# Layer-norm roots of a linear-attention and MLP block: a power on GpSimd in place of logarithm, exponential and Newton step

## The chip, the core and the metric

The kernel runs on one core of a Trainium2 chip. A core has five engines with instruction queues of their own: TensorE (PE in the profile, with its weight loads shown apart as PEld), VectorE (DVE), ScalarE (ACT), GpSimd (POOL) and SyncE (SP, which issues most DMAs). Each engine works through its queue in order and waits on semaphores for the others. The metric is the device time of one launch in microseconds. The kernel before takes 401.57 us (median of 3 runs, 401.56 to 401.84).

## What is computed

The input x has 2048 tokens of 512 channels, in fp32. It is normalised once, and the result feeds a linear attention of 32 heads and an MLP with squared ReLU; both are added to x:

```python
def _layernorm(x, axis=-1, eps=1e-5):
    m = jnp.mean(x, axis=axis, keepdims=True)
    v = jnp.var(x, axis=axis, keepdims=True)
    return (x - m) / jnp.sqrt(v + eps)

phi = lambda t: jnp.where(t > 0, t + 1, jnp.exp(t)) + 1e-6     # on q and k
kv, z = einsum("bhsd,bhse->bhde", phi(k), v), einsum("bhsd->bhd", phi(k))
o = einsum("bhqd,bhde->bhqe", phi(q), kv) / (einsum("bhqd,bhd->bhq", phi(q), z)[..., None] + 1e-6)
attention = o.reshape(B, S, D) @ wo
mlp = square(relu(xn @ w1 + b1)) @ w2 + b2
out = x + attention + mlp                                       # xn = _layernorm(x)
```

## The kernel before, in words

The tokens are cut into 16 tiles of 128 tokens (numbers 0 to 15). Every fp32 product is made of three fp32r products of a high and a low part: ScalarE copies the value to the high part (names that end in h), and VectorE or GpSimd subtracts it from the value to make the low part (names that end in l).

The program has a first stage, up to about 100 us, that walks over the 16 tiles, and a second one that walks over pairs of blocks of columns, first for one half of the tokens and then for the other. In the first stage a tile i goes through these steps:

- `measure`: VectorE's bn_stats and bn_aggr (BATCH_NORM_STATS2 and BATCH_NORM_AGGREGATE in the profile, BN_STATS and BN_AGGR in the order) give mean and variance into `mv`.
- `roots`: the root of the variance is made into the small tile `y`. Tiles are grouped, so one call serves one, two or three tiles; there are 10 groups: (0), (1), (2), (3), (4,8,9), (5,10), (6,11), (7,12), (13,14), (15).
- `normalise`: VectorE finishes the root and writes the normalised tile `xp` with one TENSOR_SCALAR of 128x512 (subtract the mean, multiply by the root).
- TensorE transposes `xp` (tiles 0 to 7) through the identity matrix `ident`; ScalarE and VectorE split the result into `xs1h`/`xs1l` or `xs0h`/`xs0l`. Tiles 8 to 15 are transposed by small DMAs (`xg`) and VectorE.
- `project` multiplies by the keys' weights (`wkh`, `wkl`, made of the loaded `rk`) into a PSUM bank `ps`; `phi` and `parts` make the keys `pk`; `tokens` makes `tok`, whose low part is a GpSimd TENSOR_TENSOR of 128x512; `kx` multiplies `pk` by `tok` into four PSUM banks `acc`.

Before the first real product TensorE runs eleven warm-up products on a tile of zeros (`zb`).

Nothing of this is issued in the order in which the code stands. All calls are recorded (class `Program`), and `order()` then plans the queues: TensorE's row is kept as it was recorded, and so is everything up to the first `kx` (the program of tiles 0 and 1 and a part of 2 to 4). For the rest, a list scheduler (`play`) with costs written by hand gives each instruction of the other engines its place; it is repeated `ROUNDS` = 500 times from each random seed in `STARTS` with due times pressed towards TensorE's gaps, and the best plan is issued. In these costs a GpSimd `tensor_tensor` and a VectorE `tensor_tensor` of SBUF operands keep each other out, and a small GpSimd instruction counts about 0.2 to 0.3 us. All instructions are issued from line 349, so the profile is read by the names of the tiles.

ScalarE's function tables are loaded once at the start (line 393, `natural_log_exp_and_others`).

Of the kernel before, what the change touches and what calls it, by code (L numbers as in the profile page):

```python
# [11 lines left out]
AF = mybir.ActivationFunctionType  # L12
OP = mybir.AluOpType
AX = mybir.AxisListType

P = 128
# [63 lines left out]
class Program:  # L80
# [96 lines left out]

    ENGINES = ("tensor", "vector", "scalar", "gpsimd", "sync")
    DEEP, FAR = 4.0, 15.0
    STARTS = (6, 14)  # L180
    ROUNDS = 500

    def order(self):
# [36 lines left out]
        plain, best, found = [t.due for t in ts], None, []  # L220
        for start in self.STARTS:
            chance, back = random.Random(start), (8, 16, 4)[start % 3]
# [138 lines left out]
def kernel(  # L361
# [12 lines left out]
    nc = Program(tc.nc)  # L374
# [67 lines left out]
    def two(name):  # L442
        return work.tile([P, 2, 512], F32, name=name, tag=next_tag("x"))

    def four(name, tag, dt=F32, pool=None):
        return (pool or work).tile([P, TB, 512], dt, name=name, tag=tag)
# [7 lines left out]
    def gjc(ap):  # L454

        return ap.rearrange("p (j g c) -> p g j c", j=NJ, g=NJ)
# [48 lines left out]
    odds = keep.tile([P, P // 2], F32, name="odds")  # L505
    b1s, zc = odds[:, 16:16 + NF], odds[:, 32:32 + 2 * NJ].rearrange("p (u j) -> p u j", u=2)
    zb = keep.tile([P, P], F32, name="zb")
    eps = odds[:, :1]

    xr, xp, xg, tok, pk, kp = {}, {}, {}, {}, {}, {}  # L510

# [204 lines left out]
    def roots(tiles, st, mv, y):  # L716

        n = len(tiles)
        nc.scalar.activation(y[:, 1, :n], mv[:, :n, 1], AF.Ln, bias=eps)
        nc.scalar.activation(y[:, 0, :n], y[:, 1, :n], AF.Exp, scale=-0.5)  # L720

    def normalise(tiles, st, mv, y):

        n = len(tiles)
        var = mv[:, :n, 1]
        y0, u, r = (y[:, k, :n] for k in range(3))

        nc.vector.scalar_tensor_tensor(u, var, 1e-5, y0, op0=OP.add, op1=OP.mult)
        nc.vector.scalar_tensor_tensor(u, u, -0.5, y0, op0=OP.mult, op1=OP.mult)
        nc.vector.scalar_tensor_tensor(r, u, 1.5, y0, op0=OP.add, op1=OP.mult)  # L730
        for k, i in enumerate(tiles):
            o, src = xp[i], xr[i]
            if i >= NPE:

                o, src = o.rearrange("p g (j c) -> p g j c", j=NJ), gjc(src)
            nc.vector.tensor_scalar(o, src, mv[:, k, 0:1], r[:, k:k + 1], op0=OP.subtract, op1=OP.mult)
            if i in groups:
                regroup(*groups[i])

    def regroup(src, G):  # L740

        for r in range(NJ):
            for g in range(NJ):
                moves.append((G[32 * g:32 * (g + 1), r], src[32 * r:32 * (r + 1), g]))
        return G
# [311 lines left out]


    nc.vector.memset(zb, 0.0)
    nc.vector.memset(eps, 1e-5)  # L1060
    t, rk = two("x0"), four("rk", "r0")
    for i in range(2):
        load_x(i, t[:, i:i + 1])
# [48 lines left out]
    for t in two_tiles:  # L1112
        roots(*t)
    normalise(*two_tiles[0])
    heads_k(0)
    high, low, keep0 = transposed(0)
    high()
    heads_k(1)
    normalise(*two_tiles[1])

    nc.gpsimd.tensor_copy(x4[:, 0, :1], two_tiles[1][3][:, 2, :1])
# [8 lines left out]
    third = statistics(2)  # L1130
    keep0()
    roots(*third)
    keep1()
    rests_k("dve", 1)
    normalise(*third)
    rests_k("dve", 3)
    fourth = statistics(3)
# [35 lines left out]
    parts(0)  # L1173
    keep2()
    roots(*fourth)
    normalise(*fourth)
    phi_k(1, pks[1])
# [68 lines left out]
    for i in range(2, NT):  # L1246
# [9 lines left out]
        k = NPE if i + 1 == NPE else i + 2  # L1256
# [463 lines left out]
```

## Time and profile before

| | before |
|---|---|
| device time, median of 3 runs | 401.57 us (401.56 to 401.84) |
| device time of the profiled execution | 402.07 us |
| its span, first to last instruction | 400.4 us |
| PE busy | 392.6 us (98%), 1763 matmul records |
| PEld busy | 324.5 us (81%) |
| DVE busy | 353.5 us (88%), 577 instructions |
| ACT busy | 271.7 us (68%), 478 instructions |
| POOL busy | 49.5 us (12%), 68 instructions |
| DMA moved | 94.37 MB, mean 236 GB/s |
| granted TensorE clock, mean | 0.997 |

Of the 402.07 us, 400.4 lie in the span and 1.7 around it. Matmuls are pipelined: a record lasts some 0.39 us, but the next one starts 0.227 us after it, so the records overlap, and TensorE waits whenever two of them start further apart than that. A share of 98% alone doesn't tell how tight the row is; the starts do. Names in the views carry no numbers, so `ps` stands for any of four PSUM banks, `acc` for any of the other four, and `y` for the small tile of any group.

### The profile page before, as it was taken

How to read it: one execution, taken by the hardware profiler on the slowest of the kernel's cores; microseconds unless marked ns; L12 is line 12 of the kernel's file. 1: busy time of each engine (PE TensorE's matmuls, PEld its weight loads, DVE VectorE, ACT ScalarE, POOL GpSimd, SP SyncE). 2: the span in 40 equal slices, each digit the busy share in tenths (PEclk: the TensorE clock that was granted, in tenths of full speed). 3: DMA queues.
4: the chain of work that ended last, by engine and by line, in shares of the span. 5: the costliest groups of instructions: out<-in, count | busy, mean ns of one | idle time of the engine just before them, and what ended most of it. 6: DMA issues, size and time to landing. Idle time of an engine off the chain costs nothing.

```text
span 400.4 us, 5611 instructions
## 1 busy us (share of the span) xinstructions
PE 392.6 (98%) x1763; PEld 324.5 (81%) x1763; DVE 353.5 (88%) x577; ACT 271.7 (68%) x478; POOL 49.5 (12%) x68
## 2 busy tenths in 40 slices
PE   7999999999999999999999999999999999999994
PEld 6778888888888887888888888887888888888884
DVE  5899999999998998999999999879999679676884
ACT  5786777677778989999757553186867677455440
POOL 2232322320122444100000000000000000000000
PEclk9999999999999999999999999999999999999998
DMA  7872387979678997797545799999975589999434
GB/s 235 289 220 58 94 249 229 338 283 310 248 230 306 327 359 275 250 315 262 186 146 199 245 235 243 306 250 255 272 232 185 178 226 292 227 281 278 156 64 95
DMA packets 80770, 94.37 MB, mean 236 GB/s; under 512 B 39490, under 2 KB 50754, under 8 KB 80484
## 3 DMA queue, kind: packets, MB, share of 16 engines
q1 hardware_dynamic: 79556, 93.49, 76.2%
q10 hardware_dynamic: 1088, 0.26, 0.3%
q0 software_dynamic: 96, 0.26, 0.3%
q8 instruction: 14, 0.23, 0.2%
q14 instruction: 16, 0.13, 0.1%
HBM read 57.81 MB, written 34.08 MB: 230 GB/s over the span
## 4 chain that ended last, share of the span: by engine, by line
PE 59%; DVE 1%; issue 0%
PE ps L349 32%; PE acc L349 28%; DVE res L349 0%; DVE o L349 0%
## 5 line engine op out<-in xcount | busy, mean ns | idle before, releaser
L349 PE MATMUL ps<-s,ops 128*128 128x512 f32 x435 | 102.6, 390 | 0.0
L349 PEld LDWEIGHTS ps<-s,ops 128*128 128x128 f32 x435 | 81.6, 188 | 17.1 <-ACT s L349 0.3
L349 DVE TENSOR_TENSOR s<-rr,s 128x512 fp32r<-128x512 f32 x56 | 38.2, 690 | 13.5 <-ACT s L349 12.9
L349 ACT ACTIVATE s<-rr 128x512 fp32r<-128x512 f32 x56 | 34.9, 630 | 22.2 <-DVE s L349 10.2
L349 PE MATMUL acc<-s,ops 128*128 128x512 f32 (+1 forms) x210 | 47.9, 380 | 0.0
L349 PE MATMUL acc<-pk,tok 128*128 128x512 f32 x192 | 47.1, 394 | 0.0
L349 PEld LDWEIGHTS acc<-s,ops 128*128 128x128 f32 x210 | 38.3, 188 | 7.5
L349 PEld LDWEIGHTS acc<-pk,tok 128*128 128x128 f32 x192 | 35.5, 188 | 7.8 <-DVE pk L349 0.6
L349 PE MATMUL acc<-T,ops 128*128 128x512 f32 x168 | 41.3, 390 | 0.0
L349 PE MATMUL ps<-T,ops 128*128 128x512 f32 x168 | 40.9, 391 | 0.1
L349 PEld LDWEIGHTS acc<-T,ops 128*128 128x128 f32 x168 | 31.5, 188 | 6.9 <-ACT rr L349 0.4
L349 PEld LDWEIGHTS ps<-T,ops 128*128 128x128 f32 x168 | 31.4, 188 | 7.0 <-ACT rf L349 0.5
L349 POOL DMA_DIRECT2D out_dram<-res x2 | 1.5, 728 | 229.0 <-DVE res L349 226.4
L349 POOL TENSOR_TENSOR tok<-xp,tok 128x512 fp32r<-128x512 f32 x16 | 21.7, 1354 | 42.1 <-ACT tok L349 30.6
L349 PE MATMUL ps<-xs0h,ops 128*128 128x512 f32 x72 | 23.7, 390 | 0.0
L349 ACT ACTIVATE rr<-acc 128x512 f32<-128x512 f32 x23 | 13.4, 586 | 12.3 <-PE acc L349 12.3
L349 DVE STREAM_TRANSPOSE d<-d 128x1024 f32<-128x1024 f32 x16 | 19.8, 1240 | 1.7 <-ACT d L349 1.5
L349 POOL TENSOR_TENSOR ops<-s,ops 128x512 fp32r<-128x512 f32 x12 | 15.9, 1328 | 25.3 <-ACT ops L349 22.2
L349 PE MATMUL acc<-xs0h,ops 128*128 128x512 f32 x56 | 18.4, 390 | 0.0
L349 ACT ACTIVATE s<-rf 128x512 fp32r<-128x512 f32 x19 | 11.9, 629 | 8.4 <-DVE rf L349 4.9
L349 ACT ACTIVATE rr<-rr,odds 128x512 f32<-128x512 f32 x15 | 10.8, 721 | 9.7 <-DVE rr L349 9.5
L349 DVE TENSOR_TENSOR ops<-raw,ops 128x512 fp32r<-128x512 f32 (+1 forms) x22 | 15.0, 681 | 2.6 <-ACT ops L349 2.6
(169 smaller groups left out, 801.4 us busy)
## 6 DMA issues: line engine op xcount, KB each, us to landing
ops<-wd SPq DMA_DIRECT2D x84, 256.0 KB, 4.1
wd<-ops SPq DMA_DIRECT2D x35, 512.0 KB, 3.6
ops<-wd SPq DMA_DIRECT2D x21, 512.0 KB, 5.8
wd<-ops SPq DMA_DIRECT2D x28, 256.0 KB, 3.5
res<-in_A_x_dram SPq DMA_DIRECT2D x32, 128.0 KB, 6.5
out_dram<-res SPq DMA_DIRECT2D x26, 128.0 KB, 3.6
ops<-wdz SPq DMA_DIRECT2D x6, 512.0 KB, 6.2
x<-in_A_x_dram SPq DMA_DIRECT2D x5, 512.0 KB, 4.9
```

Source lines behind the costliest of these rows:

```text
L349: getattr(getattr(self.nc, t.engine), t.name)(*map(real, t.args), **{k: real(a) for k, a in t.kw.items()})
```

## The change

The roots are made by two GpSimd instructions for each group: the variance plus 1e-5 into plane 1 of `y`, and that to the power of -0.5, which stands in a column of constants (`root`), into plane 2. ScalarE's Ln and Exp, and the three small VectorE instructions of the Newton step at the head of `normalise`, are gone. The scheduler starts from one random seed instead of two, so each queue is planned anew; TensorE's row is the same one.

```diff
-    STARTS = (6, 14)
+    STARTS = (5,)
...
-    eps = odds[:, :1]
+    root = odds[:, :1]
...
     def roots(tiles, st, mv, y):
         n = len(tiles)
-        nc.scalar.activation(y[:, 1, :n], mv[:, :n, 1], AF.Ln, bias=eps)
-        nc.scalar.activation(y[:, 0, :n], y[:, 1, :n], AF.Exp, scale=-0.5)
+        nc.gpsimd.tensor_scalar(y[:, 1, :n], mv[:, :n, 1], 1e-5, None, op0=OP.add)
+        nc.gpsimd.tensor_tensor(out=y[:, 2, :n], in0=y[:, 1, :n], in1=root.to_broadcast([P, n]), op=OP.pow)
 
     def normalise(tiles, st, mv, y):
         n = len(tiles)
-        var = mv[:, :n, 1]
-        y0, u, r = (y[:, k, :n] for k in range(3))
-        nc.vector.scalar_tensor_tensor(u, var, 1e-5, y0, op0=OP.add, op1=OP.mult)
-        nc.vector.scalar_tensor_tensor(u, u, -0.5, y0, op0=OP.mult, op1=OP.mult)
-        nc.vector.scalar_tensor_tensor(r, u, 1.5, y0, op0=OP.add, op1=OP.mult)
+        r = y[:, 2, :n]
...
-    nc.vector.memset(eps, 1e-5)
+    nc.vector.memset(root, -0.5)
```

GpSimd's queue at the start of the program, before (`y_147` is the root's tile of token tile 1, `wkl` a low part of the keys' weights):

```order
L349 AFFINE_SELECT heads<-heads 128x128 x2
L349 MEMSET odds 128x1
L349 MEMSET odds 1x1
L349 MEMSET xp_154 128x1
L349 COPY x_167<-y_147 128x1
L349 MEMSET xp_154 128x1
L349 TENSOR_TENSOR wkl<-rk,wkh 128x512
L349 MEMSET xp_154 128x1
L349 TENSOR_TENSOR tok_253<-xp_154,tok_253 128x512
```

And now (`y_141`, `y_150` and `y_198` belong to token tiles 0, 1 and 2, `odds` holds the constant -0.5):

```order
L349 AFFINE_SELECT heads<-heads 128x128 x2
L349 MEMSET odds 128x1
L349 MEMSET odds 1x1
L349 TENSOR_SCALAR y_141<-mv_137 128x1
L349 TENSOR_TENSOR y_141<-y_141,odds 128x1
L349 TENSOR_SCALAR y_150<-mv_144 128x1
L349 TENSOR_TENSOR y_150<-y_150,odds 128x1
L349 MEMSET xp_146 128x1
L349 COPY x_162<-y_150 128x1
L349 MEMSET xp_146 128x1
L349 TENSOR_TENSOR wkl<-rk,wkh 128x512
L349 TENSOR_SCALAR y_198<-mv_194 128x1
```

The two groups of the first two tiles stand one behind the other at the head of the queue, and the third behind the split of a weight.

VectorE's queue around token tile 4, before (`xp_378` is written for tile 4 first, `mv_269`/`y_333` belong to the group (4,8,9), `k_310` and `pk_350` to the keys of tile 2):

```order
L349 TENSOR_TENSOR xs1l<-ps_67,xs1h 128x4x128
L349 SCALAR_TENSOR_TENSOR k_310<-ps_70,k_310 128x512
L349 BN_STATS st_347<-x_167 128x6
L349 BN_STATS st_347<-x_239 128x6
L349 BN_AGGR mv_360<-st_347 128x2 x2
L349 BN_STATS st_364<-x_167 128x6
L349 SCALAR_TENSOR_TENSOR y_333<-mv_269,y_333 128x3
L349 SCALAR_TENSOR_TENSOR y_333<-y_333 128x3 x2
L349 TENSOR_SCALAR xp_378<-x_167,mv_269,y_333 128x512
L349 SCALAR_TENSOR_TENSOR pk_350<-k_310,pk_350 128x512
```

And now (the same tiles are `xp_335`, `mv_260`/`y_321`, `k_296` and `pk_338`):

```order
L349 TENSOR_TENSOR xs1l<-ps_67,xs1h 128x4x128
L349 SCALAR_TENSOR_TENSOR k_296<-ps_70,k_296 128x512
L349 TENSOR_SCALAR xp_335<-x_162,mv_260,y_321 128x512
L349 BN_STATS st_341<-x_162 128x6
L349 BN_STATS st_341<-x_230 128x6
L349 BN_AGGR mv_352<-st_341 128x2 x2
L349 BN_STATS st_356<-x_162 128x6
L349 SCALAR_TENSOR_TENSOR pk_338<-k_296,pk_338 128x512
L349 TENSOR_SCALAR xp_335<-x_162,mv_352,y_360 128x512
```

Tile 4 is now normalised right behind the keys of tile 2, ahead of three bn_stats that stood in front of it before.

## The prediction

> **What bounds the kernel now.** I read the page first, then the chain that ended last, then TensorE's own waits, and last the timeline around each of these waits. The page:
>
> ```profile
> span 400.4 us, 5611 instructions
> PE 392.6 (98%) x1763; PEld 324.5 (81%) x1763; DVE 353.5 (88%) x577; ACT 271.7 (68%) x478; POOL 49.5 (12%) x68
> PE 59%; DVE 1%; issue 0%
> ```
>
> TensorE is busy for 98% of the span, and 59% of the span is one unbroken chain of its work. The chain in order of time shows how tight that row is:
>
> ```profile
> 156.13 22.09 PE ps L349 x96
> ...
> 219.01 9.52 PE ps L349 x42
> ...
> 392.94 0.02 issue
> ```
>
> From 156.1 to 392.9 us it is TensorE without a break: 42 matmuls in 9.52 us are 0.227 us each, the pace at which one starts after the other. The 7.5 us from 392.9 to the end (400.4) are the last blocks' additions and stores. TensorE's order is the same in both programs, and the queues' last part, from where they stand at 304 us now, is the same too, so this tail stays. What the change can win or lose is therefore TensorE's waiting ahead of its work and between its matmuls. Besides the start of the warm-up, the view of its waits names three (total us, times, longest):
>
> ```profile
> PE acc L349 <- DVE y L349: 0.7, 1, 0.7
> PE acc L349 <- DVE xp L349: 0.3, 1, 0.3
> PE ps L349 <- DVE xp L349: 0.2, 1, 0.2
> ```
>
> All three wait for normalised tiles or their roots, so they are the change's business: two stand in the head (6 to 8 us), one at 26 us. Here is the head, in order of time (start, duration):
>
> ```profile
> 4.44 0.18 DVE L349 BATCH_NORM_AGGREGATE mv<-st 128x2 f32<-128x6 f32 x1
> 5.24 0.18 DVE L349 BATCH_NORM_AGGREGATE mv<-st 128x2 f32<-128x6 f32 x1
> 5.50 0.35 DVE L349 SCALAR_TENSOR_TENSOR y<-y 128x1 f32<-128x1 f32 x2
> 5.89 0.55 DVE L349 TENSOR_SCALAR xp<-x,mv,y 128x512 f32<-128x512 f32 x1
> 6.58 0.63 PE L349 MATMUL acc<-ident,xp 128*128 128x128 f32 x4 [0.68 <-DVE y L349]
> 6.92 0.55 DVE L349 TENSOR_SCALAR xp<-x,mv,y 128x512 f32<-128x512 f32 x1
> 7.24 0.60 ACT L349 ACTIVATE xs1h<-acc 128x512 fp32r<-128x512 f32 x1 [0.74 <-PE acc L349]
> 7.53 0.66 PE L349 MATMUL acc<-ident,xp 128*128 128x128 f32 x4 [0.32 <-DVE xp L349]
> 7.94 0.97 PE L349 MATMUL ps<-wkh,xs1h 128*128 128x512 f32 x2
> ```
>
> The variance of tile 0 is there at 4.62 us (4.44 + 0.18). Logarithm, exponential and Newton step take until 5.85 (5.50 + 0.35); the tile is written from 5.89 on, transposed at 6.58, split by ScalarE at 7.24, and the first real product starts at 7.94. Tile 1 follows, written at 6.92 and transposed at 7.53. Everything from 4.62 on is one chain, in which each step waits for the one before.
>
> **The change part by part. The head.** It takes ScalarE's two and VectorE's three small instructions out of this chain and puts GpSimd's two in. No power on GpSimd is in this trace. The nearest rows are these (groups of POOL instructions, then two rows of its timeline):
>
> ```profile
> L349 POOL TENSOR_TENSOR tok<-xp,tok 128x512 fp32r<-128x512 f32 x16 | 21.7, 1354 | 42.1 <-ACT tok L349 30.6 <-DVE pk L349 4.9 <-DMA wd<-ops 3.4
> L349 POOL TENSOR_TENSOR ops<-raw,ops 128x256 fp32r<-128x256 f32 x6 | 5.6, 936 | 26.9 <-ACT ops L349 26.9
> L349 POOL COPY x<-y 128x1 f32<-128x1 f32 x1 | 0.2, 184 | 0.0
> L349 POOL TENSOR_SCALAR_AFFINE_SELECT heads<-heads 128x128 f32<-128x128 f32 x2 | 0.7, 341 | 0.1
> 1.60 0.75 POOL L349 TENSOR_SCALAR_AFFINE_SELECT heads<-heads 128x128 f32<-128x128 f32 x2
> 7.32 0.19 POOL L349 MEMSET xp<- 128x1 f32 x1 [4.78 <-PE acc L349]
> ```
>
> The add is priced as the one-column COPY, 0.18 us. For the power, the least is that COPY, 0.18, and the most the 512-column TENSOR_TENSOR, 1.35. A line through 936 ns at 256 columns and 1354 at 512 has 1.63 ns per column and 0.52 us at one column; I take 0.52, since the power is a two-input TENSOR_TENSOR of one column, and an arithmetic of its own on one column is likely to be small beside the fixed part. A GpSimd instruction that waits for the one before it loses 0.07 us (two dependent selects take 0.75, not 2 x 0.341). A start behind another engine costs 0.11 (the MEMSET at 7.32, behind transposes that end at 6.58 + 0.63 = 7.21); the way back to VectorE I put at 0.04, as between VectorE's own steps (5.50 + 0.35 to 5.89).
>
> Tile 0: 4.62 + 0.11 + 0.18 + 0.07 + 0.52 + 0.04 = 5.54, against 5.89 now: 0.35 us earlier. At the power's least (0.18) it would be 5.20, but VectorE is busy with tile 1's aggregate until 5.24 + 0.18 = 5.42, so the gain is at most 0.43. Tile 1 queues behind the first power: 5.50 + 0.18 + 0.07 + 0.52 + 0.04 = 6.31, against 6.92: 0.61 earlier. Since the first product waits for the split of tile 0, the head gives 0.35. Nothing else there holds it back: the four weight loads are issued between 1.7 and 3.2 us and take at most 5.3, so the last is in by 8.5, while the last copy starts at 9.3:
>
> ```profile
> L349 SPq DMA_DIRECT2D rk<-in_A_wqkv_dram x4: 432/432/432, 1.7 to 3.2; - x4
> DMA to landing us min/median/max: 3.4/4.4/5.3
> L349 ACT ACTIVATE wkh<-rk x4: 613/627/632, 5.9 to 9.3; 128x512 fp32r<-128x512 f32 x4
> ```
>
> Two small steps of VectorE take 0.35 us in the head's rows, 0.175 each. The Trainium skill, in GPSIMD Engine Reference, section Engine selection, speaks against the move: it leaves elementwise work to VectorE, since GpSimd is about twice as slow on two inputs. As an estimate from that rule, a power of 2 x 0.175 = 0.35 us would even let the head gain its cap, 0.43, instead of 0.35; no row here has a two-input GpSimd instruction of one column, so I stay with the line through the two that there are.
>
> **The wait at 26 us.**
>
> ```profile
> 21.98 0.18 DVE L349 BATCH_NORM_AGGREGATE mv<-st 128x2 f32<-128x6 f32 x1
> 22.66 0.68 DVE L349 SCALAR_TENSOR_TENSOR k<-ps,k 128x512 f32<-128x512 f32 x1
> 25.18 1.07 PE L349 MATMUL ps<-wkh,xs1l 128*128 128x512 f32 x4
> 25.88 0.55 DVE L349 TENSOR_SCALAR xp<-x,mv,y 128x512 f32<-128x512 f32 x1
> 26.49 0.66 PE L349 MATMUL ps<-ident,xp 128*128 128x128 f32 x4 [0.24 <-DVE xp L349]
> 26.90 3.00 PE L349 MATMUL acc<-pk,tok 128*128 128x512 f32 x12
> ```
>
> The four matmuls from 25.18 on start 0.227 apart, so the next could start at 26.09; tile 4's transposes start at 26.49, when its normalisation (25.88 + 0.55 = 26.43) is over: 0.40 us of TensorE's time. Its variance was there at 22.16. In the new order this normalisation follows the keys of tile 2 (now over at 23.34), and its root is made by GpSimd at about 22.16 + 0.11 + 0.18 + 0.07 + 0.52 = 23.04. So the tile is ready near 23.9, two microseconds ahead of the transposes, and the 0.40 goes. Late next is the low part of `pk` for tile 2, which now stands behind the normalisation and three bn_stats: 23.9, three times some 0.68 (the keys' row above stands for a VectorE pass over 512 columns) and two aggregates of 0.18 make 26.3, and with a pass of its own it ends at 27.0, while TensorE, 0.40 earlier, asks for it four matmuls after its start at 26.50, at 27.4. That holds.
>
> **The other eight groups** (the third and fourth, and the pairs) have their roots hidden: TensorE shows no wait for them, and what goes there is work beside TensorE's. Here are twenty of VectorE's thirty small steps, and the busy times from 30 to 60 us (PE, PEld, DVE, ACT, POOL):
>
> ```profile
> L349 DVE SCALAR_TENSOR_TENSOR y<-y x20: 151/160/164, 5.5 to 46.1; 128x1 f32<-128x1 f32 x10, 128x2 f32<-128x2 f32 x8, 128x3 f32<-128x3 f32 x2
> 30.00:60.00 30.00, 30.00 (x140) 24.82 (x139) 28.60 (x64) 20.88 (x45) 8.56 (x14) 1.00 0.48 134
> ```
>
> Those twenty cost 20 x 0.16 = 3.2 us in all. VectorE is nearly full there (28.60 of 30), so taking work off it loosens the plan, but TensorE is busy for all of the 30 us and gains nothing. GpSimd's new instructions stand in order between the low parts of `tok`, 1.35 us each, which wait for ScalarE; a root may wait for one or two of them, and VectorE then stands still in front of that tile. That is a new coupling. GpSimd is busy for 8.56 of 30 us there, so I cost it at nothing.
>
> **The re-planned stretch** from 60 to 300 us: the view of waits names none there, but the starts show a few short ones, such as the 0.26 us between these two rows (155.64 + 0.227 = 155.87, and the next starts at 156.13):
>
> ```profile
> 155.64 0.39 PE L349 MATMUL ps<-xs1h,ops 128*128 128x512 f32 x1
> 156.13 1.66 PE L349 MATMUL ps<-T,ops 128*128 128x512 f32 x6
> ```
>
> A new plan may lose these or have others; I take no difference, with estimated bounds of -0.8 (three waits of this size gone) and +1.5 (six new ones).
>
> Sum: -0.35 - 0.40 = -0.75 us; with the power's two ends it would be -0.43 - 0.40 = -0.83 and, as worked out with the first rival, 1.04 - 0.40 = +0.64. Against the profiled execution (402.07, of which 400.4 is its span) that is 401.3. The median of the runs lies 0.5 below that execution, so the forecast for the median is 401.57 - 0.75 = **400.8 us**. A measurement of this kernel can tell about 0.2%, 0.80 us, from no change, so the forecast lies almost on that bound.
>
> **The rivals.** *The power is slow, and tile 1 pays twice (slower).* Both roots of the head stand in series on GpSimd. With a power of p, tile 1 is written at 5.26 + 2p, against 6.92, and the first product stands behind tile 1's transposes in TensorE's row. From p = 0.83 on the head loses, 2p - 1.66 (1.04 at 1.35); with the 0.40 won back, the kernel is slower from p = 1.03 on, and by over 0.80 from p = 1.43. At p = 2 it is +1.9: 403.5. For it: a power has to be computed in steps, and no row shows its arithmetic. Against: 1.43 us for one column is more than 512 columns of a subtraction take. A load of code at first use would do the same once; the only load of this kind in the trace is ScalarE's table, 1.28 us:
>
> ```profile
> L393 ACT ACT_TABLE_LOAD x1 | 1.3, 1283 | 0.8 <-PEq L1706 0.8
> ```
>
> A load of that length would write tile 1 at 6.31 + 1.28 = 7.59, 0.67 later, and the kernel would be 0.27 slower. The same page of the Trainium skill (GPSIMD Engine Reference, section Instruction dispatch) gives about 6 us for the first call to freshly loaded code, unseen in the profile; with that figure it would be some 406. In this trace no first instruction of a kind on GpSimd shows such a gap (the first COPY and the selects above), and the changed program has no load instruction that the old one lacks.
>
> *Given back in the new plan.* The gain holds to 30 us, and new waits of TensorE between 60 and 300 us eat it: 401.2 to 402.2, or in a bad plan 402.5 to 403.2. For it: all queues are reshuffled, one seed instead of two. Against: the chain has no break in that stretch worth a line, and VectorE has less to do.
>
> *More goes.* The short waits go as well: 400.8 - 0.8 = 400.0. For it: most of them end with VectorE or ScalarE, both relieved. Against: the ones after 60 us have nothing to do with the roots.
>
> **How the numbers follow.** The forecast with its small spread (-0.45 to -1.1) has 0.42, half of it on each side of the bound of 0.80; more goes, 0.18; given back within the bound, 0.17; the slow power beyond it, 0.13; a bad plan, 0.10. Faster by over 0.2%: 0.21 + 0.18 = 0.39; within: 0.21 + 0.17 = 0.38; slower: 0.23. The range from 399.9 to 403.0 takes in the case in which more goes and the milder half of the slower cases, and leaves out about 2 in 10.
>
> **What would show it.** Right: the power at 0.4 to 0.6 us; the first real product near 7.6; no wait of PE for `xp` at 26 us; 42 matmuls in 9.5 us afterwards, and the same tail of 7.5. Wrong: a power over 0.8 us and a first product later than 7.94; a wait of PE for `pk` or `xs0h` between 26 and 60 us behind a root that stands behind `tok` on POOL; or waits of over 1 us in sum after 60 us.

## The result, and the profile after

The change makes the kernel slower: 403.21 us (median of 10 runs, 402.26 to 404.42) against 401.64 us for the kernel before (10 runs beside them, 401.44 to 403.31). The ratio is 1.0033, with a 95% interval from 1.0020 to 1.0047. The forecast was 400.8 us, with a range up to 403.0.

The profiled execution took 402.32 us (402.07 before), one of the fastest of its ten. Its page:

```profile
span 400.6 us, 5579 instructions
PE 393.1 (98%) x1763; PEld 324.4 (81%) x1763; DVE 352.2 (88%) x547; ACT 267.6 (67%) x458; POOL 60.9 (15%) x88
```

Work left VectorE and ScalarE as forecast, and the 88 GpSimd instructions are busy for 11 us more; TensorE is again busy for 98%. TensorE's waits (total us, times, longest):

```profile
PE ps L349 <- DVE odds L349: 1.1, 1, 1.1
PE ps L349 <- DVE rr L349: 0.7, 1, 0.7
PE acc L349 <- DVE xp L349: 0.4, 1, 0.4
```

The first row is the warm-up's start, as before, and the third is the head's second tile. The waits for `y` and for tile 4's `xp` are gone; one for `rr`, which the kernel before hasn't, is new. The head in order of time (start, duration):

```profile
4.22 0.18 DVE L349 BATCH_NORM_AGGREGATE mv<-st 128x2 f32<-128x6 f32 x1
4.59 0.23 POOL L349 TENSOR_SCALAR y<-mv 128x1 f32<-128x1 f32 x1 [2.02 <-DVE mv L349]
4.91 0.57 POOL L349 TENSOR_TENSOR y<-y,odds 128x1 f32<-128x1 f32 x1
5.47 0.21 POOL L349 TENSOR_SCALAR y<-mv 128x1 f32<-128x1 f32 x1
5.52 0.55 DVE L349 TENSOR_SCALAR xp<-x,mv,y 128x512 f32<-128x512 f32 x1 [0.32 <-POOL y L349]
5.76 0.73 POOL L349 TENSOR_TENSOR y<-y,odds 128x1 f32<-128x1 f32 x1
6.53 0.55 DVE L349 TENSOR_SCALAR xp<-x,mv,y 128x512 f32<-128x512 f32 x1 [0.46 <-POOL y L349]
7.54 0.94 PE L349 MATMUL ps<-wkh,xs1h 128*128 128x512 f32 x2
```

From the variance (4.40) to the first product (7.54) it is 3.14 us, against 3.32 before (4.62 to 7.94): 0.18 gained, and 0.22 more because x landed earlier in this execution. At 26 us (TensorE, in order of time):

```profile
24.79 1.07 PE L349 MATMUL ps<-wkh,xs1l 128*128 128x512 f32 x4
25.70 0.60 PE L349 MATMUL ps<-ident,xp 128*128 128x128 f32 x4
```

Four matmuls 0.227 apart from 24.79 end at 25.70, and tile 4's transposes start at 25.70: the 0.40 us are won as forecast. Not all of it stays: tile 4's normalisation took 1.52 us beside GpSimd's token addition (22.93 to 24.45, where the forecast had 23.9), and TensorE stands a moment for tile 2's `pk` (over at 27.03): 0.15 us goes again by 30 us.

The 1763 matmul records of the two kernels are the same products in the same order, so their starts can be compared one by one. TensorE is 0.85 us ahead of the kernel before behind 26 us, 0.70 at 30 us and 0.50 from 52 to 137 us. The rest is lost near 138 us. GpSimd, then VectorE, then TensorE there:

```profile
134.25 2.55 POOL L349 TENSOR_TENSOR ops<-s,ops 128x512 fp32r<-128x512 f32 x2 [2.39 <-ACT ops L349]
...
135.58 2.30 DVE L349 SCALAR_TENSOR_TENSOR rr<-rr,d 128x1024 f32<-128x1024 f32 x1
...
136.32 1.52 PE L349 MATMUL ps<-T,ops 128*128 128x512 f32 x6
...
137.80 0.68 DVE L349 SCALAR_TENSOR_TENSOR rr<-ps,rr 128x512 f32<-128x512 f32 x1
...
138.53 0.50 PE L349 MATMUL ps<-xs0h,ops 128*128 128x512 f32 x1 [0.69 <-DVE rr L349]
```

The step at 137.80 empties the PSUM bank that TensorE's next product writes. Before, it ran ahead of the wide steps:

```profile
135.97 0.69 DVE L349 SCALAR_TENSOR_TENSOR rr<-ps,rr 128x512 f32<-128x512 f32 x1 [0.21 <-ACT rr L349]
```

In the new queue the 1024 wide step stands in front of it, and takes 2.30 us beside GpSimd's additions. TensorE's six matmuls are over at 137.68 (136.32 + 6 x 0.227) and it stands until 138.53. From there it is 0.4 to 0.5 us behind the kernel before, so this place cost 0.98 us. Then two things nearly cancel: the kernel before loses 0.35 us at 268 to 275 us, to a wait that the experiments explain, and the changed kernel 0.26 at 330 us. At the end it is 0.2 behind.

### The profile page after: what moved, and what is told of

It is laid out like the page before. It is cut to its first block, busy times and chain, and to the rows that moved or that the text cites. A ratio compares the mean times of both kernels' runs of the same rounds, so it can differ in the third digit from the quotient of the medians.

```text
span 400.6 us, 5579 instructions
## 1 busy us (share of the span) xinstructions
PE 393.1 (98%) x1763; PEld 324.4 (81%) x1763; DVE 352.2 (88%) x547; ACT 267.6 (67%) x458; POOL 60.9 (15%) x88
## 4 chain that ended last, share of the span: by engine, by line
PE 91%; DVE 4%; ACT 1%; issue 1%; DMA 1%; POOL 0%; DVEq 0%; POOLq 0%
PE ps L349 52%; PE acc L349 40%; DVE rr L349 1%; DVE d L349 1%; DMA x<-in_A_x_dram 1%; DVE s L349 1%; ACT rr L349 0%; POOL y L349 0%; DVE res L349 0%; DVE o L349 0%; ACT ops L349 0%; ACT d L349 0%; DVE st L349 0%; DVE h L349 0%; ACT e L349 0%
## 5 line engine op out<-in xcount | busy, mean ns | idle before, releaser
L349 POOL TENSOR_TENSOR ops<-s,ops 128x512 fp32r<-128x512 f32 x12 | 16.9, 1414 | 26.0 <-ACT ops L349 23.2
L349 ACT ACTIVATE k<-ps 128x512 f32<-128x512 f32 x16 | 9.5, 596 | 11.2 <-PE ps L349 11.1
```

The source lines that it names most:

```text
L349: getattr(getattr(self.nc, t.engine), t.name)(*map(real, t.args), **{k: real(a) for k, a in t.kw.items()})
```

## The experiments

Times are medians, with the lowest and highest run. In each series the kernels ran on one chip, beside runs of the kernel before, whose median is given. The first and third series shared a chip, the fourth and fifth another, and the second had a third one, so a small difference between two series may be the chip's. Where TensorE is said to lose or gain in a stretch, the starts of the same products in two profiled executions are compared.

**First series (before: 401.84).** Is it the power or the new plan? One kernel has the power on the old plan, one the logarithm on the new:

```diff
 # old_plan_power: the order as planned before; at emission
-scalar.activation(y1, var, Ln, bias=eps);  scalar.activation(y0, y1, Exp, scale=-0.5)
+gpsimd.tensor_scalar(y1, var, 1e-5, None, op0=add);  gpsimd.tensor_tensor(out=y2, in0=y1, in1=root, op=pow)
-three vector.scalar_tensor_tensor of the Newton step
 # new_plan_log: the order as planned after; at emission the reverse
```

> The kernel before, every instruction where its plan puts it, but ScalarE's Ln gives way to GpSimd's add, its Exp to GpSimd's power, and VectorE's Newton steps are left out. Theory A (the new plan costs, the power itself pays): PE's first product 0.2 to 0.4 us earlier than in before, the wait at 26 us gone, no new wait of PE at 138 us; the time 0.3 to 0.7 us under before, near 401.1. Theory B (the power on GpSimd costs, in series or by delaying other work): slower than before by 1 to 1.6 us, near 403. Theory C (both by halves): within 0.3 us of before.

> The changed kernel's order of all other work, but with the roots as before: Ln and Exp on ScalarE in the places of the add and the power, and the three Newton steps on VectorE ahead of each group's first normalisation. Theory A: the wait of PE near 138 us (0.85 us in the changed kernel) is there again, and the time is slower than before by 1 to 2 us, 402.6 to 403.6. Theory B: within 0.4 us of before, since the power is gone.

The power on the old plan took 401.79 us (401.14 to 402.97), ratio 0.9998 (0.9987 to 1.0009): not slower, which tells against theory B, but without the 0.3 to 0.7 us of theory A either. Its trace has the first product 0.23 us earlier and no wait at 138 us; at 26 us half of the 0.40 is left (0.21), since tile 4's normalisation still stands behind the three bn_stats there. The logarithm on the new plan took 411.87 us (409.27 to 415.25). That is no clean test: ScalarE's two steps, put into GpSimd's places, lose 5.9 us by 52 us already. It does have the same wait for `rr` of 0.7 us at 138 us, with no power in it.

Two more kernels: the pair at 136 us exchanged, and the changed kernel again.

```diff
 # swap_138: VectorE's queue
-scalar_tensor_tensor rr<-rr,d    128x1024
 scalar_tensor_tensor rr<-ps,rr   128x512
+scalar_tensor_tensor rr<-rr,d    128x1024
```

> The changed kernel with two neighbours of VectorE's queue exchanged near 136 us: the 128x512 step that empties the PSUM bank goes ahead of the 1024 wide step. Theory A (that wait is a chief part of the loss): PE's wait of 0.85 us near 138 us falls under 0.2, and the time is 0.5 to 0.9 us under the changed kernel. Theory A2 (the loss has many places): the wait goes, and under 0.3 us of it arrives at the end, as later waits take it up.

> The changed kernel once more, beside the other three on one chip: 402.3 to 404.4 us, a median 1.2 to 1.8 us above before's. If its spread is of the plan, a slower execution's trace shows waits of PE that the first profile lacks; if it is of the chip, before spreads as much.

The exchange took 402.48 us (401.46 to 404.76), the changed kernel 404.37 (402.37 to 405.69), 2.5 over before, beyond its expectation. GpSimd and VectorE in the first of them:

```profile
134.46 2.54 POOL L355 TENSOR_TENSOR ops<-s,ops 128x512 fp32r<-128x512 f32 x2 [2.40 <-ACT ops L355]
...
136.53 0.69 DVE L355 SCALAR_TENSOR_TENSOR rr<-ps,rr 128x512 f32<-128x512 f32 x1 [0.78 <-ACT rr L355]
137.13 1.22 DVE L355 SCALAR_TENSOR_TENSOR rr<-rr,d 128x1024 f32<-128x1024 f32 x1
```

The wait at 138 us is gone, and the wide step, no longer beside GpSimd, takes 1.22 us. At 138 us TensorE has won 0.96 us on the changed kernel's first execution; a new wait of 0.6 us at 146 us takes part of it, of which half is made up by 160 us. The 1.9 us between the two medians are more than this and hold the spread told next. The second execution of the changed kernel (404.56 us) shows where its spread lies. It has the same loss at 138 us, and then VectorE's wait near 255 us and TensorE at 270 us:

```profile
DVE res L349 <- DMA res<-in_A_x_dram: 2.7, 1, 2.7
```

```profile
267.79 2.43 PE L349 MATMUL acc<-T,ops 128*128 128x512 f32 x10
270.59 1.65 PE L349 MATMUL acc<-T,ops 128*128 128x512 f32 x6 [0.37 <-ACT rr L349]
...
273.21 0.39 PE L349 MATMUL acc<-xs1h,ops 128*128 128x512 f32 x1
274.35 1.66 PE L349 MATMUL acc<-T,ops 128*128 128x512 f32 x6 [0.75 <-ACT rr L349]
```

VectorE stands for the last of eight residual loads (the x that is added to the output), the chain behind it is late, and TensorE loses 0.53 us (267.79 + 10 x 0.227 to 270.59) and 0.91 (273.21 + 0.227 to 274.35). The faster execution waited 0.4 us there, the kernel before 1.6:

```profile
DVE res L349 <- DMA res<-in_A_x_dram: 1.6, 1, 1.6
```

So this wait is in both plans, and differs from run to run.

**Second series (before: 401.88, 401.43 to 404.30).** It is meant to take that wait away. Three loads of the second residual tile stand ahead of the eight in SP's queue; they go behind them.

```diff
 # SP's queue near 236 us (the changed kernel's numbers; alike in the others)
-DMA res_2367<-in_A_x_dram x3
 DMA ops<-wd_0_79;  DMA res_2388<-in_A_x_dram x4;  DMA ops<-wd_0_79;  DMA res_2388<-in_A_x_dram
 DMA ops<-wdz;  DMA res_2388<-in_A_x_dram;  DMA ops<-wd_0_79;  DMA res_2388<-in_A_x_dram x2
+DMA res_2367<-in_A_x_dram x3
```

> The changed kernel with one exchange in SP's queue: the three loads of the second residual tile that stand ahead of the eight of the first (near 236 us) go behind the last of them. Theory R (what varies from run to run is the landing of the eighth, which VectorE waits for near 255 us and, through ScalarE's evictions, PE near 272 us): it lands 1 to 2 us earlier, PE's waits at 269 to 273 us go, the wait at 138 us (0.85) stays; 402.0 to 402.6 us with runs closer together, 0.6 to 1.2 under the changed kernel. Rival S (the spread is the DMA engines' rate as a whole): the delay shows in the next loads instead and the median stays near 403.5.

> The changed kernel with both exchanges: VectorE's pair at 136 us and SP's residual loads. Theory: with both waits gone the new plan is as good as the old, 401.2 to 401.8 us. Rival: the new plan has further losses, and it stays over 402.0.

> The kernel before with the same exchange in SP's queue. Theory R: its slower runs (402 to 403.2) come from the same landing and go; its median falls to 401.3 to 401.5, 0.2 to 0.5 under before. Rival S: no difference, spread as before.

> The old plan with the power in place, and the exchange in SP's queue. Theory R: the 0.5 us that the power gives at the head is kept to the end in every run: 400.7 to 401.2 us, 0.6 to 1.0 under before, and 0.4 to 0.6 under before with the exchange. Rival S: near 401.8, as without the exchange.

| with the residual exchange | us | lowest to highest |
|---|---|---|
| after_res: the changed kernel | 403.33 | 402.83 to 404.38 |
| swap_res: and VectorE's pair exchanged | 402.45 | 401.94 to 403.04 |
| before_res: the kernel before | 401.52 | 401.29 to 401.65 |
| old_plan_power_res: the power, old plan | 401.47 | 400.96 to 401.73 |

Before_res is as theory R has it: the spread falls from 2.9 to 0.4 us, the median by 0.36, and VectorE's wait at 255 us is not in its trace. The changed kernel keeps its loss, against theory R's 402.0 to 402.6: in its trace VectorE still waits 1.7 us for the last load and TensorE loses 0.6 at 271 to 275 us, so here the exchange did not do what it was made for. The power on the old plan lies only 0.05 under before_res, against theory R's 0.4 to 0.6.

The first two rows differ by the exchange at 136 us alone, 0.88 us by their medians; part of that may be the late load, for which swap_res waited only 0.3 us. Swap_res, in which theory said 401.2 to 401.8, is still 0.98 above the power on the old plan, as its rival had it. In the two traces TensorE loses 1.0 us at 49 to 52 us, 0.6 at 146 (0.4 of it made up by 158) and 0.2 at 330, against a lead of 0.4 in its execution at 48 us. The first of these places, VectorE and GpSimd in the changed kernel and then VectorE in the kernel before:

```profile
46.08 0.71 DVE L349 STREAM_TRANSPOSE xT<-xg 128x512 f32<-128x512 f32 x1 [0.49 <-DMA xg<-xp]
46.72 0.65 DVE L349 TENSOR_TENSOR xs0l<-ps,xs0h 128x512 fp32r<-128x512 f32 x1
47.30 0.67 DVE L349 SCALAR_TENSOR_TENSOR k<-ps,k 128x512 f32<-128x512 f32 x1
47.89 0.67 DVE L349 TENSOR_TENSOR xs1l<-xT,xs1h 128x512 fp32r<-128x512 f32 x1
48.48 0.70 DVE L349 STREAM_TRANSPOSE xT<-xg 128x512 f32<-128x512 f32 x1
49.11 1.35 DVE L349 SCALAR_TENSOR_TENSOR pk<-k,pk 128x512 fp32r<-128x512 f32 x1
48.60 1.31 POOL L349 TENSOR_TENSOR tok<-xp,tok 128x512 fp32r<-128x512 f32 x1 [1.29 <-ACT tok L349]
```

```profile
47.38 0.68 DVE L349 SCALAR_TENSOR_TENSOR k<-ps,k 128x512 f32<-128x512 f32 x1
...
48.88 0.68 DVE L349 SCALAR_TENSOR_TENSOR pk<-k,pk 128x512 fp32r<-128x512 f32 x1
...
50.42 0.71 DVE L349 STREAM_TRANSPOSE xT<-xg 128x512 f32<-128x512 f32 x1 [0.52 <-DMA xg<-xp]
```

The new plan puts the turn of gathered tokens (STREAM_TRANSPOSE), which waits for a DMA, ahead of the `pk` that TensorE waits for, and `pk` takes 1.35 us instead of 0.68 beside GpSimd's token addition. In the changed kernel and in swap_138 that cost 0.2 to 0.3 us; in after_res and swap_res the turn started 0.7 to 1.0 us later, and it cost 1.0 to 1.2. Why the gathered tokens came later there is not shown.

**Third series (before: 401.66).** The kernel after_three makes the third exchange as well (to the diffs above):

```diff
 # VectorE's queue near 46 us
-stream_transpose xT<-xg
 tensor_tensor xs0l<-ps,xs0h;  scalar_tensor_tensor k<-ps,k
-tensor_tensor xs1l<-xT,xs1h;  stream_transpose xT<-xg
 scalar_tensor_tensor pk<-k,pk
+stream_transpose xT<-xg;  tensor_tensor xs1l<-xT,xs1h;  stream_transpose xT<-xg
 # ScalarE's queue: xs1h<-xT goes behind pk<-k
```

> The changed kernel with three exchanges in queues and nothing else: SP's residual loads (236 us), VectorE's pair at 136 us, and at 46 to 50 us the first two turns of gathered tokens on VectorE and the split behind the first on ScalarE, which go behind the two steps (ScalarE's and VectorE's pk) that PE waits for at 51 us. Theory Q (the whole loss is instructions that stand in a queue ahead of a step for PE): the step of 0.3 to 1.2 us at 49 to 51 us goes as well, and the time is 0.3 to 1.0 us under the kernel with two exchanges (402.45), 401.4 to 402.0. Rival T (the exchange makes PE wait for the turned tokens a little later): within 0.3 of 402.45.

It took 402.62 us (402.24 to 403.03), no better than swap_res (402.45, on another chip). The loss at 51 us is gone (TensorE is 1.1 us earlier there than in swap_res), but 0.7 of it comes back at 56 us, as rival T had it. Swap_138, on the same chip, had lost only 0.3 at 51 us, and against it the third exchange costs 0.4 by 58 us. This part of the loss is found in the trace, not undone.

The next two change only the starting numbers of the plan's random search:

```diff
 # after_old_starts                # before_new_start
-STARTS = (5,)                    -STARTS = (6, 14)
+STARTS = (6, 14)                 +STARTS = (5,)
```

> The changed kernel's tasks, planned from the two starting numbers of the kernel before (6 and 14) instead of 5. Theory L (which waits a plan leaves is chance of its search; the power takes no part in them): other waits in other places, anywhere between 401.2 and 404. Rival M (the power's tasks make every plan worse): it too lies 1.3 us or more over before, with waits behind GpSimd's instructions.

> The kernel before, planned from the starting number 5. Theory L: a different plan with the logarithm is 0.3 to 2.5 us over before as well, though no power is in it. Rival M: within 0.4 us of before.

The changed kernel from the old numbers took 402.20 us (401.02 to 403.60), ratio 1.0006 (0.9994 to 1.0019): no loss that can be told, against rival M. The kernel before from the new number took 406.67 us (405.26 to 407.21), 5.0 us worse with no power in it. Its waits begin with

```profile
PE ps L349 <- DVE rr L349: 1.3, 1, 1.3
```

and `ops`, `rf` and `s` follow with 0.6, 0.4 and 0.2. A plan of the same instructions can so differ by 5 us. Theory L has the direction; its 0.3 to 2.5 us were too little.

The last kernel of this series issues the power twice in the later groups (old plan, residual exchange):

```diff
 # power_twice_later: in groups of tiles 2 and up
+gpsimd.tensor_tensor(out=y0, in0=y1, in1=root, op=pow)   # not used
 gpsimd.tensor_tensor(out=y2, in0=y1, in1=root, op=pow)
```

> The old plan with the power and the exchange in SP's queue (401.47), and the power issued twice, one result unused, in all groups but those of the first two tiles (0.6 to 0.9 us more GpSimd work in each). The prediction's step (these groups are hidden): within 0.2 us of 401.47. Rival: they lie on the way of tile 4's transposes near 26 us or of GpSimd's token work, and the time grows by 0.5 us or more.

It took 404.07 us (403.66 to 405.01), 2.6 more than with one power (401.47, on another chip; 2.5 by the starts of the same products). GpSimd and VectorE at tile 3:

```profile
17.57 0.66 POOL L361 TENSOR_SCALAR y<-mv 128x1 f32<-128x1 f32 x1
18.31 1.09 POOL L361 TENSOR_TENSOR y<-y,odds 128x1 f32<-128x1 f32 x2
19.37 1.28 POOL L361 TENSOR_TENSOR tok<-xp,tok 128x512 fp32r<-128x512 f32 x1
```

```profile
19.44 1.50 DVE L361 TENSOR_SCALAR xp<-x,mv,y 128x512 f32<-128x512 f32 x1 [1.29 <-POOL y L361]
```

VectorE waits 1.29 us for the root, and its normalisation then falls beside GpSimd's next token addition and takes 1.50 us instead of 0.55. By 29 us all of the loss is there. On the old plan these groups are not hidden.

**Fourth series (before: 402.28, 401.57 to 403.92).** Where does the power's gain go on the old plan, and is a new plan without the residual wait good?

```diff
 # power_ahead: old_plan_power_res, GpSimd's queue at 14 to 18 us
-tensor_tensor tok<-xp,tok
 tensor_scalar y<-mv;  tensor_tensor y<-y,odds (pow)        # tile 3
+tensor_tensor tok<-xp,tok
 # power_first_two: power in tiles 0 and 1, logarithm and Newton in the rest
 # after_old_starts_res: after_old_starts, with the residual exchange
```

> The old plan with the power everywhere and the residual exchange (401.47), with one exchange in GpSimd's queue: tile 3's add and power go ahead of the token addition near 16 us, behind which they waited until 18.6 us. Theory G (the power's gain at the head is given back at tile 3, where its add stands behind 1.3 us of GpSimd work): VectorE's normalisation of tile 3 starts 0.5 to 0.8 us earlier, PE's wait of 0.2 us at 20 us goes; 401.1 to 401.4 us. Rival H: the later token addition delays PE's products by as much or more; 401.5 to 402.5.

> The old plan with the residual exchange, and the power in the groups of tiles 0 and 1 alone (a column of the constants more is set for it); all later groups keep logarithm, exponential and Newton. By theory G it has the head's 0.2 to 0.3 us and not tile 3's loss, but PE's wait at 26 us stays: 401.2 to 401.4 us. Rival: the head's gain is lost where rk lands late, and it is at 401.5 like the others.

> The changed kernel's tasks planned from the starting numbers 6 and 14, with SP's residual loads exchanged as before. Theory L with R (the loss lies in the plan, and what is left of its spread in the residual's landing): 401.0 to 401.5 us, runs close together, at or under before with the exchange (401.52). Rival M: 402 or more.

Power_ahead took 401.18 us (400.81 to 401.59), ratio 0.9974 (0.9963 to 0.9985), theory G's value. Power_first_two took 401.57 (401.41 to 401.88), ratio 0.9985 (0.9974 to 0.9996). The logarithm with the same exchange had 0.9982 (0.9968 to 0.9997) on another chip; intervals of this width can't tell the head's 0.2 us from nothing. Its trace has the head's full gain and no late weight, so its rival's reason is not shown. After_old_starts_res took 402.64 (401.27 to 403.58), ratio 1.0006, against the 401.0 to 401.5 expected: here the exchange did not help; the last residual load was still late in its profiled execution (VectorE waited 2.2 us), and TensorE lost 1.2 us at 268 to 275 us. The time is rival M's, but this wait is not GpSimd's.

**Fifth series (before: 401.97, 401.46 to 404.21).** The old plan with the residual exchange, three times on one chip:

> The kernel before with the residual exchange once more, beside the two others: 401.4 to 401.6 us.

> The same with the power in all groups. Theory G: 0 to 0.15 us under the one with the logarithm, since the head's gain is partly given back at tile 3.

> The same with tile 3's add and power ahead of the token addition. Theory G: 0.25 to 0.45 us under the one with the logarithm, near 401.15, which is what the power itself is worth where nothing is re-planned. Rival: the 401.18 of the first time was of that chip, and all three are equal within 0.1 us.

| old plan, residual exchange | us | lowest to highest | ratio to before |
|---|---|---|---|
| logarithm (before_res_2) | 401.71 | 401.46 to 401.94 | 0.9980 (0.9964 to 0.9995) |
| power (old_plan_power_res_2) | 401.30 | 401.13 to 401.55 | 0.9978 (0.9966 to 0.9990) |
| power ahead of tile 3's token addition (power_ahead_2) | 401.01 | 400.80 to 401.27 | 0.9975 (0.9964 to 0.9986) |

GpSimd and VectorE at tile 3 with the power:

```profile
15.86 1.30 POOL L361 TENSOR_TENSOR tok<-xp,tok 128x512 fp32r<-128x512 f32 x1 [2.44 <-ACT tok L361]
17.12 0.67 POOL L361 TENSOR_SCALAR y<-mv 128x1 f32<-128x1 f32 x1
17.87 0.58 POOL L361 TENSOR_TENSOR y<-y,odds 128x1 f32<-128x1 f32 x1
```

```profile
18.48 0.55 DVE L361 TENSOR_SCALAR xp<-x,mv,y 128x512 f32<-128x512 f32 x1 [0.78 <-POOL y L361]
```

and with the add and power ahead, GpSimd, then VectorE:

```profile
13.77 0.22 POOL L368 TENSOR_SCALAR y<-mv 128x1 f32<-128x1 f32 x1 [0.50 <-DVE mv L368]
14.07 0.57 POOL L368 TENSOR_TENSOR y<-y,odds 128x1 f32<-128x1 f32 x1
15.69 1.29 POOL L368 TENSOR_TENSOR tok<-xp,tok 128x512 fp32r<-128x512 f32 x1 [1.04 <-ACT tok L368]
```

```profile
17.45 0.54 DVE L368 TENSOR_SCALAR xp<-x,mv,y 128x512 f32<-128x512 f32 x1
```

Tile 3's variance is there at 13.7 us, and the token addition in front of the add itself waited for ScalarE until 15.86. With the two exchanged the normalisation starts 1.03 us earlier, without a wait. The add alone takes 0.22 us instead of 0.67, the latter beside VectorE's `pk`.

On the old plan the power was thus worth 0.41 us on this chip (401.71 to 401.30; the ranges overlap by 0.09), after 0.05 in the second series, and tile 3's exchange 0.29 more. All three expectations missed: the logarithm was to take 401.4 to 401.6, the power to win at most 0.15 and the two steps together at most 0.45, where they won 0.70. Theory G has the place and the direction, but not the size: by the starts of the same products the power loses only 0.08 us to the logarithm at tile 3 (20 to 24 us), and the exchange wins 0.3 there, most of which the logarithm did not have either. Power_ahead_2 is 0.96 us under the kernel before of its series (401.97), with the residual exchange in it; both kernels of the change are slower.

## Why the prediction was wrong

The step that failed is the re-planned stretch, of which the prediction says: "I take no difference, with estimated bounds of -0.8 (three waits of this size gone) and +1.5 (six new ones)". Its zero should have been about +1.9: from the power on the old plan with the residual exchange (401.47) to the changed kernel with it (403.33) it is 1.86 us. Two things in that step were wrong. The waits were sized by one of 0.26 us, and a single one, at 138 us, cost 0.98 in the trace (0.88 between the medians with and without it). And the stretch was begun at 60 us, though the new plan moves work before that: 0.2 us was lost at 49 to 52 us in the first execution and 1.2 in after_res, where the prediction had costed the roots alone and said that TensorE "gains nothing". After_res also lost 0.6 to a late residual load and 0.2 at 330 us, whose cause is not shown. The time went the way of "given back in the new plan", the rival with 0.27 in two parts, to the worse end of its bad plan (403.2).

- **Head, -0.35.** The mechanism held, the size not: 0.18 us from variance to first product (3.32 to 3.14; 3.13 to 3.16 in twelve of the fifteen profiled executions with the power, 3.31 to 3.47 in the five with the logarithm). That the product came near 7.6 us as forecast is in part luck, since x landed 0.22 earlier. GpSimd started 0.19 behind VectorE's end, not 0.11; the add took 0.23, not 0.18; the power 0.57 and 0.73, not 0.52. The slow-power rival, which needed 0.83, did not come.
- **"Nothing else there holds it back".** Not in every execution: TensorE's own pace and the first weight did. In three of the fifteen executions with the power the product came 0.07 to 0.34 us later than in the others (3.21, 3.35 and 3.48 us from the variance); the rows stand below.
- **The wait at 26 us, -0.40.** Right as a term. The `pk` behind it, of which the prediction says "That holds", came a moment late, and 0.15 us was lost again by 30 us.
- **"The other eight groups have their roots hidden", cost nothing.** Wrong at tile 3, if by little: the coupling was named there, a root behind `tok` on POOL, and priced at nothing because GpSimd was seldom busy. VectorE stood 0.78 us for that root in the changed kernel too, and TensorE lost 0.07 at 20 to 24 us; the better order was worth 0.29 on the old plan. What counted was the queue's order at one place.
- **The sum of the local terms, -0.75,** came near what the power gave where nothing is re-planned and tile 3's add goes first: 401.71 to 401.01, -0.70. That is in part luck: by the traces 0.2 of it is the head's and 0.2 to 0.3 that of 26 us, and as much comes from tile 3, which the sum did not have.
- **The base, 401.57.** Three runs hid that the kernel before spreads up to 403 to 404, for a residual load's landing.

The rows to the second point are the weight loads of tile 0's four transposes, in the first execution of the changed kernel and in its second:

```profile
6.12 0.42 PEld L349 LDWEIGHTS acc<-ident,xp 128*128 128x128 f32 x4 [0.22 <-DVE xp L349]
```

```profile
6.17 0.71 PEld L349 LDWEIGHTS acc<-ident,xp 128*128 128x128 f32 x4 [0.27 <-DVE xp L349]
```

TensorE's first products of 128 columns (the warm-up, then these transposes) start 0.21 us apart, and from some moment on 0.11 apart; the moment lay between 4.3 and 6.9 us. With the power the transposes come earlier, and in three executions they started ahead of it; in none of the five with the logarithm. In the second execution the last transpose ends at 7.25, ScalarE's split of the result starts at 7.29, and the first product at 7.94, where 7.60 would have followed from the variance there (4.46 + 3.14). The first weight was late there too: ScalarE's copy of it, which began between 5.01 and 6.51 us in the twenty profiled executions, took from 6.51 to 7.14. In old_plan_power_res, where this copy was over at 6.63, the slow transposes alone made it 3.35 us from variance to product.

What stays open: why after_res and after_old_starts_res keep their late residual, why the power on the old plan was worth 0.05 us in one series and 0.41 in another, and whether the loss near 51 us can be undone, since the exchange there made another wait. One rival is untested: the plan's costs count a small GpSimd instruction 0.2 to 0.3 us, and the power took 0.57 to 0.89, so truer costs might find a better plan. The plan from the old numbers, made with the same costs, shows no loss that can be told.

## What to carry to other kernels

Where a search orders the whole program, a small edit is two changes, the edit and a new plan: emit the edit in the old order first, and compare plans of unchanged work to learn what a plan is worth (here up to 5 us, for an edit worth 0.4 at most). A wait of the critical engine is found in the queue that feeds it: ask what stands ahead of the step it waits for, and when that becomes ready, not how busy the engine is. Several profiled executions of one kernel show which wait makes its spread, and that wait may be the better thing to mend.

## What the runs showed of the hardware

The power on GpSimd costs 0.14 to 0.18 us more for each further column, by these groups (busy us, mean ns):

```profile
L349 POOL TENSOR_TENSOR y<-y,odds 128x1 f32<-128x1 f32 x5 | 3.1, 610 | 0.4
L349 POOL TENSOR_TENSOR y<-y,odds 128x2 f32<-128x2 f32 x4 | 3.0, 750 | 0.3
L349 POOL TENSOR_TENSOR y<-y,odds 128x3 f32<-128x3 f32 x1 | 0.9, 892 | 0.1
```

The means hold calls that ran beside VectorE's normalisation (0.73 us at one column, 0.86 at two); the others took 0.57 to 0.61 and 0.71. The line from which the prediction took 0.52 us has 1.63 ns per column. The Trainium skill (GPSIMD Engine Reference, section Engine selection) puts GpSimd at about half VectorE's speed on two inputs, for add, multiply and maximum; by some 570 ns against the 159 of a one-column Newton step on VectorE a power is beyond that, 3.6 times. The first power shows no load of code (0.57 us).

VectorE's steps with both inputs in SBUF, and its normalisation from SBUF to SBUF, hardly advance while a GpSimd two-input instruction runs. The 1024 wide step began at 135.58, 0.08 after GpSimd's (135.50 to 136.80), and took 2.30 us; alone it takes 1.22, and 136.80 + 1.22 is 138.02, close to its end at 137.88. A normalisation took 1.50 instead of 0.55, and ended 0.26 before such a sum (19.37 + 1.28 + 0.55 = 21.20, against 20.94). The step `rr<-ps,rr`, with one input in PSUM, took its usual 0.69 beside such an instruction (swap_138, where GpSimd's ran until 137.0). The Trainium skill (SBUF — State Buffer, section SBUF: two separate sides) says that the two engines share one pair of ports, which for such steps whoever starts first holds for its whole instruction; the rows agree to 0.14 and 0.26 us.
